# Keys and queries of an attention batch loaded ahead of its values, with block sums and value products later in TensorE's order

## The chip, the cores and the metric

One core of one Trainium2 chip runs the kernel. The metric is device time in microseconds (us) of one execution. The kernel before was run three times: 496.35, 497.45 and 497.51 us, median 497.45. The names of the profile are used: PE is TensorE, PEld its weight loads, DVE is VectorE, ACT is ScalarE, POOL is GpSimd, SP is SyncE, whose queue (SPq) issues nearly all DMAs of the attention stage.

## The reference

Three layers follow each other: an attention with a window and block summaries, a mixture of experts in which each token goes to one expert of limited capacity, and a second feed-forward layer with a gated softmax and a normalization. The change touches the attention alone. Batch is 2, heads 8, sequence 768, head dimension 64.

```python
k_sum = k.reshape(B, H, nb, block, D).max(axis=3)      # block = 32, nb = 24
v_sum = v.reshape(B, H, nb, block, D).mean(axis=3)
scores_l = scale * np.matmul(q, k.transpose(0, 1, 3, 2))
mask_l = np.abs(pos[:, None] - pos[None, :]) < window   # window = 16
scores_s = scale * np.einsum('bhsd,bhnd->bhsn', q, k_sum)
scores_s = scores_s + np.log(block)
scores_l_m = np.where(mask_l, scores_l, -1000000000.0)
scores_all = np.concatenate([scores_l_m, scores_s], axis=-1)
scores_all = scores_all - np.max(scores_all, axis=-1, keepdims=True)
a = np.exp(scores_all)
a = a / (np.sum(a, axis=-1, keepdims=True) + 1e-09)
v_all = np.concatenate([v, v_sum], axis=2)
return np.matmul(a, v_all).astype(np.float32)
```

Every query therefore sees its near keys and the 24 block summaries of all blocks; the product with the values takes the near values and the 24 block means of the values.

## The kernel before

The attention is cut into 24 units: 2 batches, 4 pairs of heads, 3 groups of four tiles of 64 queries. A unit passes three steps on TensorE. `score` (L332) multiplies the queries of two heads with 96 near keys and 24 block maxima; DVE adds the mask and takes the minimum (L338), ACT takes the exponential (L341). `attnT` (L348) transposes the weights and ACT copies them to a tile aT (L350). `pv` (L361) multiplies them with Vw, which holds for each tile 96 near values and in 24 further rows the block means; DVE divides by the sum (L364, L365, L368).

Before the first unit of a pair of heads, `prep` brings its keys and queries into the layout that the scores need, in three steps: DVE or POOL reorder the loaded keys kn into kr (L276), TensorE transposes keys (L292) and queries (L300), DVE copies the keys and takes block maxima (L294, L313), ACT copies the queries into qbd (L303), and DVE or POOL fill the summaries and margins of kTw (L315, L320, L321). Three pairs of such tiles exist, and three load buffers each for keys and queries.

The block means of the values come from `vsum`, once for a batch. Its first step sums the blocks by twelve products with all values of the batch (L255). Its second step lets ACT copy the sums (L259), moves them by one product to the right partitions (L261), lets ACT copy them again to a tile vs (L263), and issues eight DMAs on SP, one for each head (L265), that write them into the 24 rows of Vw. So a `pv` needs the values of its tiles and, of its own two heads, the two DMAs of L265.

TensorE and SP do what the code says in the order in which it says it: a table `plan` gives each step a place on a scale on which score u stands at u, and the steps are written out sorted by it. The order on DVE, ACT and POOL is made by the scheduler. What is written before the plan, as the first loads, stands first. In the plan of before, `pv` of unit u stands at the later of u + 3.5 and 5.3 + u/2, the two steps of `vsum` at 3.29 and 3.89 for batch 0 and at 12.65 and 13.25 for batch 1, and the loads of batch 1 among the units from 3 on.

When the attention ends, the tokens x go to memory (L372) and through `xT` (L382) and `logits` (L394) to the gating scores L. Then routing begins (`head`, L138 and following), after a memset (L823) in memory that the attention's tiles had held. During the last units three parts of the weight w_in are split into a high and a low half (`split64`, L70 to L79), with the tile ch between.

Of the kernel before, what the change touches and what calls it, by code (L numbers as in the profile page):

```python
# [8 lines left out]
F32 = mybir.dt.float32  # L9
F32R = mybir.dt.float32r  # L10
BF = mybir.dt.bfloat16
I32 = mybir.dt.int32
# [9 lines left out]
def tile_attention_moe_solu(ctx, tc, q, k, v, w_gate, w1, w2, w_in, w_out, g_ln, out):  # L22
# [6 lines left out]
    HP = H // 2  # L29
    NT = S // 64  # L30
    NBK = S // 32
    WIN = 96
    KEYS = WIN + NBK
# [29 lines left out]
    def split64(cv, raw, hi, lo, after=None, late=None):  # L63
        n = hi.shape[1]
        with tc.high_priority(-3000):
            y = cv.tile([128, n], F32, name="cy")
            h = cv.tile([128, n], I32, name="ch", bufs=2)

            with tc.issue_after(after.ins) if after is not None else nullcontext():
                nc.scalar.activation(y, raw[:, :, 1].bitcast(F32), AF.Abs, scale=2.0 ** -112)  # L70
            with tc.issue_after(late.ins) if late is not None else nullcontext():
                nc.vector.tensor_scalar(h, y.bitcast(I32), 3, 0x3FFFFFF8, op0=OP.logical_shift_left,
                                        op1=OP.bitwise_and)
            nc.vector.scalar_tensor_tensor(h, raw[:, :, 1], -0x40000000, h, op0=OP.bitwise_and, op1=OP.bitwise_or)
            nc.vector.scalar_tensor_tensor(h, raw[:, :, 0], 29, h, op0=OP.logical_shift_right, op1=OP.bitwise_or)
            h = h.bitcast(F32)
            nc.scalar.copy(hi, h)
            for c in range(0, n, 256):
                nc.gpsimd.tensor_tensor(lo[:, c:c + 256], h[:, c:c + 256], hi[:, c:c + 256].bitcast(F32), op=OP.subtract)  # L79
# [89 lines left out]
    cva = att.enter_context(tc.tile_pool(name="cva", bufs=1))  # L169
    ld = att.enter_context(tc.tile_pool(name="ld", bufs=3))  # L170
    vp = att.enter_context(tc.tile_pool(name="vp", bufs=1))
    wk = att.enter_context(tc.tile_pool(name="wk", bufs=2))
# [5 lines left out]
    def load_qk(b, hp):  # L178
        for nm, src in (("k", k), ("q", q)):
            t = ld.tile([128, 2, 3, 2 * D], F32, name=nm + "n")  # L180
            dma(t, src[b, 2 * hp:2 * hp + 2].rearrange("h (c p r) d -> p h c (r d)", c=3, r=2))
            nat[nm, b, hp] = t
# [3 lines left out]
    def load_v(b, t):  # L186
        lo = max(0, 64 * t - 16)
        hi = min(S, 64 * t + 80)
        o = lo - (64 * t - 16)
        dma(Vw[o:o + hi - lo, b, t, :, 0:D], v[b, :, lo:hi, :].rearrange("h p d -> p h d"))  # L190
# [23 lines left out]
    for i in range(NB):  # L214
        a = vp.tile([128, NT, KEYS], F32, name=f"kTw{i}")
# [8 lines left out]
    nc.vector.memset(Vw[0:32, :, 0, :, 0:D], 0.0)  # L224
    nc.vector.memset(Vw[64:96, :, NT - 1, :, 0:D], 0.0)
    load_qk(0, 1)
    for t in range(NT):
        load_v(0, t)
        if t == 5:
            load_qk(0, 2)  # L230
    for hp in range(3, HP):
        load_qk(0, hp)
    dma(wg, w_gate.rearrange("(k p) e -> p k e", p=128))

    nc.gpsimd.memset(Vw[:, :, :, :, D], 1.0)
# [108 lines left out]
    def attnT(u):  # L344
        s = ST.pop(u)
        p = pa.tile([128, 4, 128], F32, name="pA", bufs=2)
        for n in range(4):
            nc.tensor.transpose(p[0:KEYS, n, :], s[:, n, :], ident)  # L348
        a = wk.tile([KEYS, 4, 128], F32, name="aT", bufs=6)
        nc.scalar.copy(a, p[0:KEYS])  # L350
        AT[u] = a

# [48 lines left out]
    def at(u, f, *a):  # L401
        plan.setdefault(u, []).append((f, a))

    for u in range(NU):
        b, hp, g = units[u]
        i = b * HP + hp
        at(u, score, u)
        at(u + (2.2 if u < 21 else 1.9), attnT, u)
        at(max(u + (3.5 if u < 21 else 3.3), 5.3 + u / 2), pv, u)
    for i in range(1, B * HP):  # L410
        u0 = units.index((*divmod(i, HP), 0))
        for g in range(3):
            if i == 1:
                at(g + 0.4, prep, 0, 1, g)
            else:
                at(max(u0 + g - 4.5, g + 2.9), prep, *divmod(i, HP), g)
    for st in range(2):
        at(3.29 + 0.6 * st, vsum, 0, st)
        at(12.65 + 0.6 * st, vsum, 1, st)
    for b in range(B):  # L420
        for g in range(3):
            for n in range(2):
                u = units.index((b, HP - 1, g)) + (4 if b else 5.4)
                at(u + 0.7 * n + .6, xT, b * JB + 2 * g + n)
                at(u + 0.7 * n + 1.7, logits, b * JB + 2 * g + n)
    for t in range(NT):
        at(5 + t / 3, load_v, 1, t)
    for hp in range(HP):
        at(3 * hp + 3, load_qk, 1, hp)
    at(16, routing_consts)  # L430
    NCA = 3
    RAW64 = {}
# [5 lines left out]
    def split_in(cv, i, *after):  # L438
        kk, hf = divmod(i, 2)
        split64(cv, RAW64.pop(i), wiH[:, kk, 512 * hf:512 * hf + 512], wiL[:, kk, 512 * hf:512 * hf + 512], *after)  # L440
# [396 lines left out]
    def split_out(cv, i, after):  # L837
        split64(cv, RAW64.pop(8 + i), woH[:, i], woL[:, i], after)
# [53 lines left out]
    for ph in range(E):  # L892
        u = 540 if ph > WHOLE else 650
# [63 lines left out]
```

## Time and profile before

| what | value |
|---|---|
| median of three runs | 497.45 us |
| the profiled execution's own time | 498.66 us |
| its span, first to last instruction | 497.0 us |
| PE busy | 447.6 us, 90% of the span |
| PEld busy | 387.7 us, 78% |
| DVE busy | 274.3 us, 55% |
| ACT busy | 176.0 us, 35% |
| POOL busy | 89.0 us, 18% |
| chain that ended last | PE 71%, DVE 12%, DMA 6%, ACT 5% |
| mean granted clock of TensorE | 0.968 of full speed |

The attention fills about the first 104 us of the span, the routing of the first expert the stretch to 128 us, and the experts and the last layer the rest. The busy shares are means over stages with different limits. For a change in the attention the table says only that TensorE is busy most of the time; which engine ends last in that stage is read from the stretch itself.

### The profile page before, as it was taken

The numbers are of one execution on the slowest core, as the hardware profiler recorded it, in microseconds if no ns is written. First come the engines' busy times: TensorE is split into PE (matmuls) and PEld (weight loads), VectorE is DVE, ScalarE is ACT, GpSimd is POOL, SyncE is SP. The second block draws the span as 40 slices with busy tenths as digits, with TensorE's granted clock in tenths as the row PEclk, the third lists the DMA queues.
The fourth block names the chain that finished last, engine by engine and source line by source line (L and its number), as shares of the span: only waits on it lengthen the run. The fifth ranks groups of instructions, "written<-read, shape, count | busy, mean of one in ns | idle before, by whom it ended". The sixth has DMA issues, their size and how long they took to land.

```text
span 497.0 us, 9767 instructions
## 1 busy us (share of the span) xinstructions
PE 447.6 (90%) x3723; PEld 387.7 (78%) x3723; DVE 274.3 (55%) x1033; ACT 176.0 (35%) x425; POOL 89.0 (18%) x150
## 2 busy tenths in 40 slices
PE   2799999845778988999999999999999999999995
PEld 1668688634678868789888988988898899998773
DVE  7658577878594697675256526626662322213441
ACT  3578778711233432331321413123141313222331
POOL 9311200302324243202000200200020110100012
PEclk9999999975798998999999999999999999999999
DMA  9979861363869159008304800740390560000001
GB/s 195 195 158 207 220 181 40 109 231 131 272 218 368 54 180 316 1 2 279 113 1 137 257 21 1 243 149 1 118 275 30 179 205 1 1 22 1 22 21 42
DMA packets 92463, 64.61 MB, mean 130 GB/s; under 512 B 25728, under 2 KB 87168, under 8 KB 92416
## 3 DMA queue, kind: packets, MB, share of 16 engines
q1 hardware_dynamic: 90432, 57.70, 41.2%
q0 software_dynamic: 1984, 6.29, 3.5%
q8 instruction: 29, 0.48, 0.4%
q14 instruction: 18, 0.15, 0.1%
HBM read 56.51 MB, written 6.29 MB: 126 GB/s over the span
## 4 chain that ended last, share of the span: by engine, by line
PE 71%; DVE 12%; DMA 6%; ACT 5%; issue 3%; SPq 1%; POOL 0%; POOLq 0%; DVEq 0%; ACTq 0%
PE m L694 28%; PE h L759 13%; PE o L802 11%; PE pS L332 4%; PE pO L361 2%; DVE ge L124 2%; DMA xg<-xd,oidx 2%; PE pr L502 2%; PE pA L348 1%; DVE ex L768 1%; DMA wl<-in_moe_w_dram 1%; DMA kn<-in_k_dram 1%; PE tr L666 1%; ACT s L341 1%; PE T L255 1%
## 5 line engine op out<-in xcount | busy, mean ns | idle before, releaser
L694 PE MATMUL m<-xs,wr 128*128 128x192 f32 x384 | 79.7, 341 | 1.2 <-ACT xs L672 1.1
L694 PEld LDWEIGHTS m<-xs,wr 128*128 128x128 f32 x384 | 65.2, 195 | 6.2 <-ACT xs L672 1.4
L742 DVE TENSOR_TENSOR yl<-m,yh 128x128 fp32r<-128x128 f32 (+1 forms) x64 | 16.2, 253 | 82.1 <-ACT yh L741 82.1
L711 ACT ACTIVATE hT<-m 128x192 f32<-128x192 f32 x64 | 21.2, 331 | 90.0 <-PE m L694 76.6
L694 PE MATMUL m<-hT,wh 128*128 128x192 f32 x256 | 51.7, 332 | 0.0
L694 PE MATMUL m<-hT,wl 128*128 128x192 f32 x256 | 50.7, 335 | 0.0
L694 PEld LDWEIGHTS m<-hT,wl 128*128 128x128 f32 x256 | 45.0, 195 | 3.3
L694 PEld LDWEIGHTS m<-hT,wh 128*128 128x128 f32 x256 | 44.5, 193 | 3.7
L741 ACT CAST yh<-m 128x128 fp32r<-128x128 f32 (+1 forms) x64 | 15.2, 238 | 88.9 <-PE m L694 80.6
L341 ACT ACTIVATE s<-s,mx 128x120 f32<-128x120 f32 x96 | 31.5, 387 | 13.6 <-DVE mx L338 13.4
L759 PE MATMUL h<-wiH,yh 128*128 128x512 f32 x96 | 34.4, 446 | 0.0
L332 PE MATMUL pS<-kTw,qbd 128*128 128x120 f32 x192 | 27.8, 290 | 5.8 <-DVE kTw L315 4.8
L777 POOL TENSOR_TENSOR st<-st,mhalf 128x1 f32<-128x1 f32 x12 | 6.9, 574 | 144.8 <-DVE st L776 104.8
L759 PE MATMUL h<-wiL,yh 128*128 128x512 f32 x96 | 32.3, 424 | 0.0
L759 PE MATMUL h<-wiH,yl 128*128 128x512 f32 x96 | 32.2, 424 | 0.0
L802 PE MATMUL o<-woH,lh 128*128 128x512 f32 x96 | 30.8, 432 | 1.3 <-ACT lh L791 1.3
L802 PE MATMUL o<-woL,lh 128*128 128x512 f32 x96 | 32.0, 429 | 0.0
L332 PEld LDWEIGHTS pS<-kTw,qbd 128*128 128x128 f32 x192 | 24.8, 202 | 7.6 <-issue 6.0
L124 DVE TENSOR_TENSOR ge<-e,ios 128x1536 bf16<-128x1536 bf16 (+3 forms) x37 | 29.7, 803 | 0.8
L802 PE MATMUL o<-woH,ll 128*128 128x512 f32 x96 | 29.4, 418 | 0.0
L764 DVE TENSOR_REDUCE st<-h 128x1 f32<-128x1024 f32 x12 | 14.7, 1224 | 26.4 <-PE h L759 26.4
L338 DVE CUSTOM_DVE_ANT_0 s<-pS,mask 128x120 f32<-128x120 f32 x96 | 21.4, 278 | 12.4 <-PE pS L332 5.5
(184 smaller groups left out, 823.5 us busy)
## 6 DMA issues: line engine op xcount, KB each, us to landing
wr<-in_moe_w_dram SPq DMA_DIRECT2D x24, 512.0 KB
wl<-in_moe_w_dram SPq DMA_DIRECT2D x20, 512.0 KB
wh<-in_moe_w_dram SPq DMA_DIRECT2D x20, 512.0 KB
raw<-in_moe_w_in_dram SPq DMA_DIRECT2D x8, 512.0 KB
raw<-in_moe_w_out_dram SPq DMA_DIRECT2D x8, 512.0 KB
Vw<-in_v_dram SPq DMA_DIRECT2D x20, 192.0 KB
kn<-in_k_dram SPq DMA_DIRECT2D x8, 384.0 KB
qn<-in_q_dram SPq DMA_DIRECT2D x8, 384.0 KB
```

Source lines behind the costliest of these rows:

```text
L124: nc.vector.tensor_tensor(out, x.rearrange("p (j t) -> p j t", t=2)[:, :, None, :].to_broadcast([128, n // 2, b - a, 2]), ios[:, None, a:b ...
L332: nc.tensor.matmul(p[:, n, :], qbd[i][:, t, :], kTw[i][:, t, :], start=True, stop=True)
L338: nc.vector.tensor_tensor_reduce(s[:, n, :], p[:, n, :], m, scale=1.0, scalar=3.0e38, op0=OP.add, op1=OP.min, accum_out=mx[:, n:n + 1])
L341: EXPS[u] = nc.scalar.activation(s[:, n, :], s[:, n, :], AF.Exp, bias=mx[:, n:n + 1], scale=-1.0)
L361: nc.tensor.matmul(p[o:o + 64, n // 2, h, :], a[:, n, 64 * h:64 * h + 64], Vw[:, b, t, 2 * hp + h, :], start=True, stop=True)
L694: nc.tensor.matmul(p[:, :CAP], w[:, d, o:o + 128], rhs[:, d], start=d == 0, stop=d == n - 1)
L711: after(ph, "h", f, nc.scalar.activation(h[:, f], p[:, :CAP], AF.Relu))
L741: a = nc.scalar.copy(hi, s[:, s0:s0 + n])
L742: nc.vector.tensor_tensor(YL[k][:, d, c:c + n], s[:, s0:s0 + n], hi.bitcast(F32), op=OP.subtract)
L759: nc.tensor.matmul(ps, a[:, d, :], w[:, d, 512 * s:512 * s + 512], start=n == 0, stop=n == len(mm) - 1)
L764: nc.vector.tensor_reduce(st[:, 0:1], p, axis=AX.X, op=OP.max)
L802: nc.tensor.matmul(p, a[:, f, :], w[:, f, :], start=n == 0, stop=n == len(mm) - 1)
```

## The change

The diff, without unchanged parts:

```diff
-            h = cv.tile([128, n], I32, name="ch", bufs=2)
+            h = cv.tile([128, n], I32, name="ch", bufs=1 if cv is cva else 2)
...
     load_qk(0, 1)
-    for t in range(NT):
+    load_qk(0, 2)
+    for t in range(4):
         load_v(0, t)
-        if t == 5:
-            load_qk(0, 2)
-    for hp in range(3, HP):
-        load_qk(0, hp)
     dma(wg, w_gate.rearrange("(k p) e -> p k e", p=128))
...
-        a = wk.tile([KEYS, 4, 128], F32, name="aT", bufs=6)
+        a = wk.tile([KEYS, 4, 128], F32, name="aT", bufs=8)
...
-        at(max(u + (3.5 if u < 21 else 3.3), 5.3 + u / 2), pv, u)
+
+        at(max(u + (3.5 if u < 21 else 3.3), 9.05 + u / 2 if u < 12 else 10.1 + 0.57 * u), pv, u)
...
-                at(max(u0 + g - 4.5, g + 2.9), prep, *divmod(i, HP), g)
+                at(max(u0 + g - (4.5 if i < 4 else 3.4), g + 2.9), prep, *divmod(i, HP), g)
     for st in range(2):
-        at(3.29 + 0.6 * st, vsum, 0, st)
-        at(12.65 + 0.6 * st, vsum, 1, st)
+        at(7.63 + 0.6 * st, vsum, 0, st)
+        at(15.25 + 0.6 * st, vsum, 1, st)
...
+    at(0.02, load_qk, 0, 3)
+    for t in range(4, NT):
+        at(0.03, load_v, 0, t)
+    for i, u in ((4, 3), (5, 6), (6, 9.02), (7, 12)):
+        at(u, load_qk, *divmod(i, HP))
     for t in range(NT):
-        at(5 + t / 3, load_v, 1, t)
-    for hp in range(HP):
-        at(3 * hp + 3, load_qk, 1, hp)
+        at(9 if t < 6 else 9.03, load_v, 1, t)
```

The loads of the third pair of heads go ahead of the values of batch 0, and the fourth pair after the first four value tiles. The block sums of batch 0 go from behind score 3 to behind score 7, and the first product with the values from behind score 5 to behind score 9. In batch 1 the sums go from behind score 12 to behind score 15, and the products with the values stand later up to unit 15. Two more tiles aT hold the weights that wait for their product; the room comes from one tile ch.

On TensorE before, the place of the block sums of batch 0 and of the first product with the values. kr and qn are the keys and queries of a pair of heads, s the weights, comb the matrix of the second step; L255 and L261 are the two steps of the sums:

```order
L348 MATMUL pA<-ident,s 120x128 x4
L255 MATMUL T<-Vw,ind 32x512 x12
L261 MATMUL T<-s_358,comb 24x512
L292 MATMUL T<-ident,kr 128x128 x2
L300 MATMUL T<-ident,qn 128x128 x3
L332 MATMUL pS<-kTw_136,qbd_137 128x120 x4
L348 MATMUL pA<-ident,s 120x128 x4
L292 MATMUL T<-ident,kr 128x128 x4
L300 MATMUL T<-ident,qn 128x128 x3
L332 MATMUL pS<-kTw_136,qbd_137 128x120 x4
L348 MATMUL pA<-ident,s 120x128 x4
L361 MATMUL pO<-Vw,aT 64x65 x8
```

The same place on TensorE in the changed kernel (its lines are three lower: L252 and L258 are the sums, L358 is the product with the values):

```order
L252 MATMUL T<-Vw,ind 32x512 x12
L329 MATMUL pS<-kTw_142,qbd_143 128x120 x4
L345 MATMUL pA<-ident,s 120x128 x4
L258 MATMUL T<-s_523,comb 24x512
L289 MATMUL T<-ident,kr 128x128 x4
L329 MATMUL pS<-kTw_130,qbd_131 128x120 x4
L358 MATMUL pO<-Vw,aT 64x65 x8
L345 MATMUL pA<-ident,s 120x128 x4
L358 MATMUL pO<-Vw,aT 64x65 x8
```

Between the second step of the sums and the first product stood eight groups of products; now there stand two, the transposes of one key step and one score. A score and a transpose now stand between the two steps of the sums.

On DVE before, from the copies of the second pair's keys to the first mask operation of the first score:

```order
L276 COPY kr<-kn 128x3x128 x2
L294 COPY kTw_130<-T 128x8x64
L294 COPY kTw_130<-T 128x4x64
L313 TENSOR_REDUCE ks<-kTw_130 128x24
L320 COPY kTw_130<-kTw_130 128x11x16
L321 COPY kTw_130<-kTw_130 128x11x16
L315 COPY kTw_130<-ks 128x12x24
L338 ISA s,mx<-pS,mask_109 128x120
```

The same on DVE in the changed kernel:

```order
L273 COPY kr<-kn 128x3x128 x2
L291 COPY kTw_130<-T 128x8x64
L291 COPY kTw_130<-T 128x4x64
L273 COPY kr<-kn 128x3x128
L310 TENSOR_REDUCE ks<-kTw_130 128x24
L317 COPY kTw_130<-kTw_130 128x11x16
L318 COPY kTw_130<-kTw_130 128x11x16
L273 COPY kr<-kn 128x3x128
L312 COPY kTw_130<-ks 128x12x24
L335 ISA s,mx<-pS,mask_109 128x120
```

The two copies of the third pair's keys now stand among the operations that the first score waits for; before they stood behind the masks of score 1.

On SP in the changed kernel, the queue from the loads of the second half of batch 0 to the first loads of w_in:

```order
L262 DMA Vw<-vs 24x12x64 x8
L190 DMA Vw<-in_v_dram 80x8x64
L190 DMA Vw<-in_v_dram 96x8x64 x5
L181 DMA kn<-in_k_dram 128x6x128
L181 DMA qn<-in_q_dram 128x6x128
L190 DMA Vw<-in_v_dram 96x8x64 x5
L190 DMA Vw<-in_v_dram 80x8x64
L181 DMA kn<-in_k_dram 128x6x128
L181 DMA qn<-in_q_dram 128x6x128
L369 DMA xd<-x 128x2x512 x3
L60 DMA raw<-in_moe_w_in_dram 128x1024
L262 DMA Vw<-vs 24x12x64 x8
```

All values of batch 1 stand behind the eight DMAs of the sums of batch 0, as before, and those of the sums of batch 1 now stand behind two pairs of key and query loads, three stores of x and one load of w_in. Before, they stood behind three pairs and one store.

## Rows read from the trace of the kernel before

**Rows 1.** Busy time of each engine in stretches of 10 us, with columns.
```profile
core 0: us, PE busy (x) PEld busy (x) DVE busy (x) ACT busy (x) POOL busy (x), PEclk, DMA share, GB/s
20.00:30.00 10.00, 7.68 (x53) 3.65 (x52) 5.19 (x25) 6.78 (x16) 0.42 (x1) 1.00 1.26 220
30.00:40.00 10.00, 10.00 (x125) 8.90 (x125) 8.30 (x42) 9.40 (x23) 2.47 (x6) 1.00 0.55 113
40.00:50.00 10.00, 10.00 (x128) 9.04 (x126) 8.27 (x47) 8.76 (x24) 1.88 (x5) 1.00 1.10 209
50.00:60.00 10.00, 10.00 (x104) 6.28 (x104) 5.76 (x34) 7.72 (x19) 2.37 (x6) 1.00 1.02 249
```
**Rows 2.** TensorE in order of time, first score to first value product.
```profile
13.96 2.04 PE L332 MATMUL pS<-kTw,qbd 128*128 128x120 f32 x8 [4.77 <-DVE kTw L315]
...
20.99 0.66 PE L292 MATMUL T<-ident,kr 128*128 128x128 f32 x4 [0.20 <-ACT qbd L303]
22.68 1.12 PE L332 MATMUL pS<-kTw,qbd 128*128 128x120 f32 x8 [1.03 <-ACT qbd L303]
...
24.17 3.01 PE L255 MATMUL T<-Vw,ind 96*32 96x512 f32 x24
27.85 1.04 PE L261 MATMUL T<-s,comb 128*24 128x512 f32 x2 [0.67 <-ACT s L259]
...
29.56 0.55 PE L300 MATMUL T<-ident,qn 128*128 128x128 f32 x3 [0.30 <-ACT vs L263]
...
33.45 0.73 PE L361 MATMUL pO<-Vw,aT 120*64 120x65 f32 x16
```
**Rows 3.** TensorE in order of time, a steady stretch of units.
```profile
41.61 1.05 PE L332 MATMUL pS<-kTw,qbd 128*128 128x120 f32 x8
42.49 0.60 PE L348 MATMUL pA<-ident,s 128*120 128x128 f32 x4
43.02 0.73 PE L361 MATMUL pO<-Vw,aT 120*64 120x65 f32 x16
...
49.34 1.05 PE L332 MATMUL pS<-kTw,qbd 128*128 128x120 f32 x8
```
**Rows 4.** The end of the attention on TensorE, in order of time.
```profile
92.34 0.70 PE L361 MATMUL pO<-Vw,aT 120*64 120x65 f32 x16 [1.25 <-ACT s L341]
...
95.08 0.33 PE L382 MATMUL pA<-ident,x 128*128 128x128 f32 x1 [0.31 <-DVE x L368]
...
97.77 0.33 PE L382 MATMUL pA<-ident,x 128*128 128x128 f32 x1 [0.79 <-DVE x L368]
```
**Rows 5.** Pieces of the chain that ended last: start, us, what.
```profile
98.28 5.31 DMA xd<-x
...
124.61 3.01 DMA xg<-xd,oidx
```
**Rows 6.** VectorE in order of time, its copies of loaded keys.
```profile
8.07 3.02 DVE L276 COPY kr<-kn 128x384 f32<-128x384 f32 x2 [1.50 <-DMA kn<-in_k_dram]
...
19.12 0.74 DVE L276 COPY kr<-kn 128x384 f32<-128x384 f32 x2
...
27.30 0.75 DVE L276 COPY kr<-kn 128x384 f32<-128x384 f32 x2 [2.44 <-DMA kn<-in_k_dram]
```
**Rows 7.** ScalarE in order of time, last copy of the block sums.
```profile
28.93 0.58 ACT L263 COPY vs<-T 24x512 f32<-24x512 f32 x1 [1.13 <-PE T L261]
```
**Rows 8.** The issues of the block sums' DMAs on SP.
```profile
29.53 6.97 SPq L265 DMA_DIRECT2D Vw<-vs  x8
```
**Rows 9.** VectorE in order of time, the split of w_in (L74, L75).
```profile
94.94 0.68 DVE L74 SCALAR_TENSOR_TENSOR ch<-raw,ch 128x512 int32<-128x512 int32 x1
...
95.65 0.69 DVE L75 SCALAR_TENSOR_TENSOR ch<-raw,ch 128x512 int32<-128x512 int32 x1
```
**Rows 10.** Engines by stretch at the end of the attention and in routing.
```profile
88.00:98.00 10.00, 7.65 (x108) 6.13 (x103) 8.57 (x36) 7.13 (x17) 4.21 (x6) 1.00 0.30 107
107.00:117.00 10.00, 2.80 (x55) 1.93 (x55) 6.71 (x35) 0.66 (x1) 0.00 (x0) 0.50 0.40 143
```

## The prediction

> **What bounds the kernel now.** I read the busy time in stretches first. From 30 to 60 us TensorE is busy for 10.00 of 10.00 us in every stretch, while ScalarE has 7.72 to 9.40 and VectorE less [rows 1]; so from there the attention lasts as long as TensorE's work, and a new order gains nothing in that stretch. From 20 to 30 us TensorE has 7.68: here an order can gain. The second view is TensorE in order of time [rows 2]. After the first score at 13.96 us it stands for 0.20 and 1.03 us (queries that ScalarE copies), then, around the block sums, 0.67 us (ScalarE's copy of the sums) and 0.30 us. That is 2.20 us in all until the first value product at 33.45 us. The block sums themselves (3.01 and 1.04 us) stand early, but they are work and not waits; moving them moves it. The third view is the end of the stage [rows 4]: 1.25, 0.31 and 0.79 us, together 2.35 us. The stage ends with the last tokens' store, 5.31 us from issue to landing, behind which the chain goes on into routing [rows 5]; beside it run the last transposes and gating scores. Everything after that is one chain through routing, which the change doesn't touch, so a shift of the attention's end is passed on whole. At most 2.20 + 2.35 = 4.55 us can be gained, if no new wait comes.
>
> **The change part by part**, as time of TensorE until the attention's end.
>
> *Loads.* The keys of the third pair land before the values, and with them the 2.44 us goes for which VectorE stood for the fourth pair's keys [rows 6]. That wait ended no wait of TensorE of its own, since TensorE was at the block sums meanwhile; its worth is in the 0.30 us above. The price is on VectorE's order: the two copies of the third pair's keys now stand before the first score. In their old place they took 0.74 us [rows 6], so the first score comes 0.7 us later. The least is 0, the most 3.0 us, as two such copies took at 8.07 us, where POOL worked beside them. I take 0.7, since it is the same pair's row.
>
> *Block sums later.* With a score and a transpose between the steps, ScalarE's copy is covered: 0.67 and 0.30 us go, and I count the 0.20 with them: -1.2. The 1.03 us stay, for the first queries' copies stand as they did.
>
> *Units without value products.* A steady unit takes (49.34 - 41.61) / 3 = 2.58 us on TensorE, of which the value product is some 0.7 [rows 3]; without it 1.9. ScalarE has 8.76 us of work in 10 us [rows 1], so 2.25 us for a unit. In the five units from score 3 to the sums, TensorE would run ahead by at most 5 x 0.35 = 1.8 us. The transposes stand 2.2 units behind their score, which absorbs most of it; what is left is that a transpose of queries needs a buffer that ScalarE empties. Bounds 0 and 1.8; I take 0.6, about one copy by ScalarE as in rows 7.
>
> *First value product.* It needs the means of its two heads in Vw. Before, from the end of the second step (27.85 + 1.04 = 28.89 us) to the product at 33.45 us passed 4.56 us [rows 2]. Eight groups of products filled them, so TensorE did not stand. In these 4.56 us lie ScalarE's copy, 0.58 us [rows 7], and two issues of 6.97 / 8 = 0.87 us each [rows 8], after the second of which the landing follows. The bounds of that path are 0.58 + 2 x 0.87 = 2.3 us, if landing were free, and 4.56. Nearest in kind is the small gather, 3.01 us from issue to landing [rows 5]: 0.58 + 0.87 + 3.01 = 4.5, which I take. In the changed order only a key step (0.66 [rows 2]) and a score (49.34 - 41.61 is three units; score to transpose 42.49 - 41.61 = 0.88 [rows 3]) stand between: 1.5 us. New wait: 4.5 - 1.5 = 3.0 us (bounds 0.8 and 3.1). Behind the waiting product stand all other steps of TensorE; ScalarE and VectorE run dry, for their next scores come from there. The products of units 1 and 2 need no more DMAs, and from unit 3 the DMAs have had a unit's time for each.
>
> By this wait TensorE works in some 7 of 10 us, as at the end of the stage, where it had 7.65 of 10 us and the granted clock stayed at 1.00; with 2.80 of 10 in routing it was 0.50 [rows 10]. I therefore add nothing for the clock. The Trainium skill (TensorE: Matmul & The Clock Gate, "The HAM clock gate") says that the array's clock follows how busy it was recently and halves when it idles, which speaks against this change; the row at 88 us shows gaps without such a fall, that at 107 us shows the fall. By the page alone one would add work at half speed behind the wait, which the first rival below prices.
>
> *Sums of batch 1.* The copy of the sums frees a buffer that the second query transpose behind it needs: 0.5 us, from 0.58 [rows 7] (bounds 0 and 0.6). Then seven groups stand before the first product of batch 1: a score, two transposes of x and two gating scores, a transpose, queries. At 0.88 for the score, 0.53 for a transpose (43.02 - 42.49 [rows 3]) and some 0.4 for the small ones this is 3.5 us against 4.5: 1.0 us of wait. On top may come the queue of transfers. From the end of batch 0's issues, near 46 us, twelve value tiles (10 x 192 + 2 x 160 KB), four key or query loads of 384 KB, and three stores and one load of 512 KB stand ahead: 5.8 MB, at 209 to 249 GB/s [rows 1] 24 to 28 us, so they land between 70 and 74 us. TensorE comes to the place at about 72 us. The wait lies between 0 and 3.3 us; I take 1.2.
>
> *End of the stage.* ScalarE now copies the last two transposed weight tiles ahead of the third part of the split, and VectorE does the second split behind the value products: I count the 1.25 and the 0.31 us as gone, and half of the 0.79. Against it the third split's two operations, 0.68 and 0.69 us [rows 9], now stand within the head of routing: +1.0 after their overlap with the store. Together -0.9 (bounds -2.35 and +1.4).
>
> The sum: 0.7 - 1.2 + 0.6 + 3.0 + 0.5 + 1.2 - 0.9 = +3.9 us. The profiled execution took 498.66 us, its span 497.0 and 1.7 around it, and lies 1.2 us above the median of 497.45; I add the sum to both: 502.6 for such an execution, 501.4 for the median. The tiles aT and the smaller ch cost nothing else: two more aT are what eight waiting units need, and the one ch only binds the splits to each other, counted at the end.
>
> **The rivals.**
> *A heavier wait.* The 3.0 us stop brings the clock to its lower level for a stretch, or the copies before the first score take their 3.0 us. For it: the fall in routing, and the row at 8.07 us. Against it: 1.00 with 7.65 of 10 busy. Doubled work for as long as the stop costs 3 us more: 504.4. Chance 0.10.
> *An exchange.* Without the transfers' queue (-1.2), with ScalarE's lag absorbed (-0.6) and the end at half of its bound (-0.3), 1.8 us are left, and if landing takes 1 us less than the gather's, 0.8: 498.2, no difference that can be told. For it: the small sum of waits on both sides. Chance 0.20.
> *Faster.* ScalarE was the second bound, with 6.78 of 10 us before 30 us and 9.40 after [rows 1]. Eight units of exponentials before the first value product use its idle time, and later no unit waits for ScalarE: all waits at the end go (-2.35) with the early ones (-1.2), and the first product finds its means because ScalarE's lag lets TensorE come there late. 0.7 - 3.55 + 0.5 = -2.4: 495.1. It decides from a wait at the first product under some 0.7 us. Against it: TensorE is back to back from 30 us already, so ScalarE isn't what it waits for, and a late arrival is itself time. Chance 0.17.
> The forecast has 0.53.
>
> **How the numbers follow.** A measurement tells a difference from about 0.3%, 1.5 us. The forecast and the heavier wait are slower: 0.63. The exchange is the same: 0.20. The rest is faster: 0.17. The range goes from 496.6, which takes in the exchange and leaves the faster case out, to 504.8 with the heavier wait.
>
> **What would show it.** Right: the first score near 14.7 us; no wait at the sums' second step; one wait of TensorE of about 3 us at the first value product, put down to the DMAs of the sums or to nothing that the profile shows; one of 1 to 3 us at the first product of batch 1; the last store some 4 us later. Wrong: a first value product without a wait, or waits at the end that vanish altogether; or a routing that shifts by another amount than the last store, for then the later stages answer too. If the clock falls in the attention, the first rival holds.

## The result and the profile after

The changed kernel took 504.49 us (median of four runs, 501.83 to 506.09), the kernel before, with one run more than was shown, 497.48 us. The ratio is 1.0139, 95% interval 1.0092 to 1.0186: 4.6 to 9.3 us slower. The forecast was 501.4 us with a range of 496.6 to 504.8. The profiled execution took 504.62 us, its span 502.9 against 497.0. One later run, of e1 at 509.93 us, was in the slower state that some executions of a kernel show; it is left out of its median and ratio.

TensorE after, in order of time from the first score to the first value product (start us, us, engine, line, operation, in brackets the idle time before it and what ended it). Lines of the attention are three lower than before: L358 is the value product, L252 and L258 the block sums.

```profile
14.48 2.03 PE L329 MATMUL pS<-kTw,qbd 128*128 128x120 f32 x8 [5.29 <-DVE kTw L312]
...
23.48 1.12 PE L329 MATMUL pS<-kTw,qbd 128*128 128x120 f32 x8 [1.15 <-ACT qbd L300]
...
27.93 0.55 PE L297 MATMUL T<-ident,qn 128*128 128x128 f32 x3 [0.58 <-ACT qbd L300]
...
30.74 0.55 PE L297 MATMUL T<-ident,qn 128*128 128x128 f32 x3 [0.72 <-ACT qbd L300]
...
34.19 2.79 PE L252 MATMUL T<-Vw,ind 96*32 96x512 f32 x24
...
39.18 1.04 PE L258 MATMUL T<-s,comb 128*24 128x512 f32 x2 [0.68 <-ACT s L256]
...
43.60 0.33 PE L358 MATMUL pO<-Vw,aT 120*64 120x65 f32 x2 [1.91 <-DMA Vw<-vs]
44.51 1.14 PE L358 MATMUL pO<-Vw,aT 120*64 120x65 f32 x14 [0.57 <-DMA Vw<-vs]
...
48.85 1.90 PE L329 MATMUL pS<-kTw,qbd 128*128 128x120 f32 x8
...
104.47 0.66 PE L379 MATMUL pA<-ident,x 128*128 128x128 f32 x4 [0.47 <-ACT xT L384]
...
112.08 0.34 PE L503 MATMUL pr<-oh,ge 128*16 128x8 bf16 x8 [1.11 <-DVE L L393]
```

Against [rows 2] the reader sees four things. The first score is 0.52 us later. The wait of 0.30 us behind the sums is gone, but that of 0.67 us at their second step is there as before, and two waits of 0.58 and 0.72 us for ScalarE's query copies are new. The first value product waits 1.91 and then 0.57 us for the sums' DMAs: together the 2.48 us that take the place forecast at 3.0. And the score at 48.85 us takes 1.90 us, where [rows 3] have 1.05. Why shows the view by stretches (busy us with instruction counts, then the granted clock, DMA share and GB/s):

```profile
core 0: us, PE busy (x) PEld busy (x) DVE busy (x) ACT busy (x) POOL busy (x), PEclk, DMA share, GB/s
30.00:40.00 10.00, 8.60 (x69) 5.43 (x68) 4.40 (x31) 9.71 (x24) 2.84 (x7) 1.00 0.24 61
40.00:44.00 4.00, 2.02 (x15) 1.55 (x14) 1.59 (x9) 2.79 (x8) 0.00 (x0) 1.00 0.17 35
44.00:51.00 7.00, 6.49 (x53) 5.71 (x55) 2.82 (x9) 1.61 (x3) 1.04 (x3) 0.51 0.49 101
51.00:60.00 9.00, 9.00 (x137) 7.85 (x134) 7.20 (x43) 6.44 (x17) 0.96 (x2) 1.00 1.29 223
```

From 30 to 40 us ScalarE is the engine that works all the time (9.71 of 10), where TensorE was in [rows 1]. TensorE then stands for about half of the stretch from 40 to 44 us, and behind that stop the granted clock is 0.51, the lower of its two levels (1.2 GHz), while TensorE has full work. Before, the clock was 1.00 all through the attention.

Where the time to the first routing product (112.08 against 103.51 us) comes from, worked out from all TensorE rows between: its idle time and its work from the first score to the end of the last value product, and the rest. "Again" are second profiles of the unaltered kernels, from the experiments.

| profile | first score | idle | work | last product to routing | first routing product |
|---|---|---|---|---|---|
| before | 13.96 | 3.87 | 78.24 | 7.44 | 103.51 |
| before again | 12.24 | 3.70 | 78.48 | 7.81 | 102.23 |
| after | 14.48 | 6.83 | 82.10 | 8.67 | 112.08 |
| after again | 14.23 | 7.20 | 78.79 | 7.75 | 107.97 |

### The profile page after: what moved, and what is told of

Same layout as the page of the kernel before. It is cut to its first block, busy times and chain, and to the rows that moved or that the text cites. A ratio compares the mean times of both kernels' runs of the same rounds, so it can differ in the third digit from the quotient of the medians.

```text
span 502.9 us, 9771 instructions
## 1 busy us (share of the span) xinstructions
PE 448.3 (89%) x3723; PEld 388.6 (77%) x3723; DVE 275.9 (55%) x1033; ACT 176.3 (35%) x425; POOL 87.0 (17%) x150
## 4 chain that ended last, share of the span: by engine, by line
PE 66%; DVE 12%; ACT 8%; DMA 5%; issue 4%; SPq 2%; POOL 1%; POOLq 0%; DVEq 0%; ACTq 0%
PE m L695 27%; PE h L760 13%; PE o L803 11%; PE pS L329 3%; ACT s L338 3%; PE pO L358 2%; DMA xg<-xd,oidx 2%; DVE ge L124 2%; PE pr L503 2%; DMA kn<-in_k_dram 1%; ACT qbd L300 1%; DMA wl<-in_moe_w_dram 1%; PE pA L345 1%; DVE ex L769 1%; SPq L631 1%
## 5 line engine op out<-in xcount | busy, mean ns | idle before, releaser
L695 PE MATMUL m<-hT,wh 128*128 128x192 f32 x256 | 50.6, 327 | 0.0
L695 PE MATMUL m<-hT,wl 128*128 128x192 f32 x256 | 49.0, 327 | 0.0
L695 PEld LDWEIGHTS m<-hT,wl 128*128 128x128 f32 x256 | 43.4, 189 | 3.2
L329 PEld LDWEIGHTS pS<-kTw,qbd 128*128 128x128 f32 x192 | 26.1, 211 | 8.9 <-issue 8.7
```

The source lines that it names most:

```text
L329: nc.tensor.matmul(p[:, n, :], qbd[i][:, t, :], kTw[i][:, t, :], start=True, stop=True)
L695: nc.tensor.matmul(p[:, :CAP], w[:, d, o:o + 128], rhs[:, d], start=d == 0, stop=d == n - 1)
```

## The experiments

Times are medians; every ratio compares the mean with that of runs of the kernel before on the same chip, with its 95% interval. The kernel before took 496.3 to 498.0 us on these chips, so versions are compared by their ratios. "Wait" is the idle time of TensorE at the first value product, "routing" the start of the first routing product. "Half clock" is the time at the lower clock, before and after 100 us of the span: the sum of 5 us x 2 x (1 - granted clock) over stretches of 5 us from 10 to 300 us. It counts time at the lower level, not what that costs.

| kernel | us | ratio | first score | wait | routing | half clock |
|---|---|---|---|---|---|---|
| before | 497.48 | | 13.96 | 0 | 103.51 | 0 + 30.7 |
| before again (e9) | 497.97, one run | | 12.24 | 0 | 102.23 | 0 + 34.1 |
| after | 504.49 | 1.0139 [1.0092, 1.0186] | 14.48 | 2.48 | 112.08 | 6.8 + 27.3 |
| after again (e5) | 504.51 | 1.0142 [1.0093, 1.0191] | 14.23 | 2.48 | 107.97 | 0 + 34.1 |
| e1, wait filled | 505.28 | 1.0113 [1.0049, 1.0176] | 14.47 | 0.21 | 107.64 | 0 + 37.6 |
| e2, sums early | 500.64 | 1.0058 [1.0024, 1.0093] | 14.22 | 0.26 | 104.96 | 0 + 34.2 |
| e3, loads only | 499.52 | 1.0035 [1.0004, 1.0066] | 14.47 | 0 | 104.08 | 0 + 34.2 |
| e4, two ch | 506.01 | 1.0173 [1.0136, 1.0211] | 14.50 | 2.48 | 109.70 | 6.8 + 27.2 |
| e6, orders only | 506.24 | 1.0172 [1.0111, 1.0233] | 12.27 | 3.63 | 112.74 | 10.3 + 27.3 |
| e7, sums late | 511.91 | 1.0304 [1.0242, 1.0367] | 14.47 | 9.51 | 117.76 | 10.2 + 27.3 |
| e8, copies on POOL | 497.78 | 1.0040 [1.0003, 1.0077] | 13.40 | 0.26 | 105.71 | 0 + 27.4 |
| e10, small dose | 505.49 | 1.0162 [1.0117, 1.0208] | 14.23 | 2.87 | 110.37 | 3.4 + 34.1 |
| e11, copies on ScalarE | 499.53 | 1.0057 [1.0030, 1.0084] | 12.26 | 0.25 | 104.59 | 0 + 34.1 |
| e12, values first | 497.92 | 1.0031 [1.0011, 1.0050] | 12.24 | 0.25 | 104.26 | 0 + 34.1 |

**e1: the wait filled with work.** Ten products that nothing reads, ahead of the first value product:

```
+    def busy(n):
+        p = pa.tile([128, 512], F32, name="T", bufs=2)
+        for i in range(n):
+            nc.tensor.matmul(p[:, 0:128], ident, ident, start=True, stop=True)
...
     def pv(u):
         b, hp, g = units[u]
         a = AT.pop(u)
+        if u == 0:
+            busy(10)
```

> The changed kernel with ten products that nobody reads (identity by identity, some 2.5 us) on TensorE ahead of the first value product: the wait for the block sums stays, but TensorE is busy in it. Theory of the clock: of the changed kernel's loss, some 2.5 us is the wait itself and some 3.9 us the granted clock of 0.5 behind it, from 44 to 51 us. Then the clock stays at 1.00 there, the first value product comes at about 44 us as before, and the time is 3 to 4 us under the changed kernel's, about 501. Rival: the extra busy time of TensorE comes from its new order and not from the clock; then nothing moves, 504 to 505.

The products took 2.50 us (from 40.83 us) and the wait was 0.21 us; the clock stayed at 1.00 until 106.2 us, and routing began 4.4 us earlier than after. But the time was not better, against the theory's 501, and its half-clock stretches behind 100 us were 37.6 us. In this profile the fall is gone with the stop; in the next run it is gone with the stop left whole, so that the products kept the clock up is not shown.

**e5: the changed kernel again**, unaltered.

> The changed kernel once more, unaltered, to see which of its readings repeat. Theory: the waits are set by its order, so the wait at the first value product comes again at 2.3 to 2.7 us, the first score at 14.3 to 14.7 us, and the last transposes' and the routing's head's waits within 0.3 us. The granted clock behind the wait falls to 0.5 in some executions and not in others: chance one half here; with the fall the first routing product starts near 112 us, without it near 108 to 109.5. Rival: the fall belongs to this order whatever the run, so it comes again with the product at 112 us. Time 503.5 to 505.5 on either, since later stages' half-clock stretches move the other way.

TensorE again, at the first value product and at the start of routing:

```profile
43.28 0.33 PE L358 MATMUL pO<-Vw,aT 120*64 120x65 f32 x2 [1.91 <-DMA Vw<-vs]
44.17 0.69 PE L358 MATMUL pO<-Vw,aT 120*64 120x65 f32 x14 [0.57 <-DMA Vw<-vs]
...
107.97 0.34 PE L503 MATMUL pr<-oh,ge 128*16 128x8 bf16 x8 [1.44 <-DVE L L393]
```

```profile
40.00:50.00 10.00, 7.52 (x101) 6.47 (x101) 6.07 (x30) 5.98 (x16) 1.03 (x3) 1.00 0.38 79
```

The waits at the value product are the same to 0.01 us and the clock did not fall: same order, same stop, 2.52 of 5 us busy from 40 to 45 us in both (from 40 to 50 us 7.52 in both, with a clock of 0.71 after). The fall is a matter of the execution. Routing came 4.1 us earlier here, the end of the span only 1.3 us (501.6 against 502.9). The 2.8 us between can be placed: e5 has two stretches at the lower level, 3.4 us each, that the first profile of after lacks. First after, then e5:

```profile
160.00:165.00 5.00, 3.46 (x23) 3.02 (x21) 2.68 (x8) 1.53 (x5) 1.89 (x3) 1.00 1.11 367
190.00:195.00 5.00, 3.20 (x29) 2.50 (x28) 5.00 (x21) 1.14 (x4) 1.24 (x2) 1.00 0.94 304
```

```profile
160.00:165.00 5.00, 4.10 (x20) 3.97 (x19) 0.89 (x3) 1.95 (x5) 1.41 (x2) 0.70 1.10 376
190.00:195.00 5.00, 3.11 (x33) 2.63 (x32) 4.97 (x19) 1.02 (x3) 2.58 (x3) 0.77 1.09 377
```

Its lead on TensorE is 4.5 us at 150 us of the span, 2.8 at 169 and 1.4 at 221: 1.7 and 1.5 us go where these stretches lie. So in this pair each fall has its price; after paid for one in the attention and e5 for two behind it, and the sum of half clock is 34.1 us in both.

**e2: sums early.** After, with the sums of batch 0 about where they cover the path:

```
-        at(7.63 + 0.6 * st, vsum, 0, st)
+        at(6.03 + 0.6 * st, vsum, 0, st)
```

> The changed kernel with the block sums of batch 0 at 6.03 and 6.63 instead of 7.63 and 8.23, all else as it is: between their second step and the first value product then stand two scores, three transposes and a key step, about 4.4 us, as long as the sums need to get into place. Theory of wait and clock: the wait of 2.5 us shrinks to under 0.5, the clock stays at 1.00, and 5 to 6 us of the loss go: 498 to 500. Rival, that the loss lies in the loads and the late order of all value products: only the wait goes, 502.

The wait shrank to 0.26 us, routing began 3.0 us earlier than in e5 (2.2 of it this wait, 0.7 that at the sums' second step, which is gone), and the ratio fell from 1.0139 to 1.0058; the time lies between the theory's 498 to 500 us and the rival's 502. The late place of the sums is the largest single part of the loss, and 0.2 to 0.9% remain without it.

**e7 and e10: sums later**, the same line with 8.44 and with 8.39.

> The changed kernel with the two steps of the sums of batch 0 directly before the first value product (8.44 and 9.04 in place of 7.63 and 8.23), the opposite direction of the run with early sums. Theory: the cover between the second step and the product was a key step of 0.66 us and a score of 0.88 to 1.05, in sum 1.6; without it the wait at the first value product grows from 2.5 to about 4.0 us, the clock falls behind it in its profile, and time is 505.5 to 507.5. Rival (the wait is not the path's but the DMA queue's, busy with values and keys at that moment): the wait stays near 2.5 us and the time with it.

Both theories failed: the wait was 9.31 and then 0.20 us. At 9.04 the second step had come behind the twelve value loads of batch 1, which stand at 9 and 9.03, and a pair of keys and queries at 9.02; SP issues in the order of the code. Its last issues up to the sums' in e7:

```profile
37.73 0.81 SPq L181 DMA_DIRECT2D qn<-in_q_dram  x1
38.58 7.37 SPq L190 DMA_DIRECT2D Vw<-in_v_dram  x6
46.05 6.78 SPq L262 DMA_DIRECT2D Vw<-vs  x8
```

The eight issues of the sums started at 46.05 us, as the loads were out. ScalarE's copy for them was ready at 42.56 us (41.98 + 0.58), and after, with a free queue, the issues began 0.02 us behind that copy: 3.5 us of the wait are the queue. The transfers were slower too: from the first issue to the value product 5.2 us here, with a DMA share of 1.24 meanwhile, against 2.7 us after, with 0.18. The dose had moved more than one thing. e10 keeps SP's order and takes only the key step out of the cover:

> The changed kernel with the two steps of the sums of batch 0 at 8.39 and 8.99 in place of 7.63 and 8.23, so that between the second step and the first value product only one score (0.9 to 1.1 us) is left and no key step, with SP's order unchanged: the small dose that the run before, in which the sums' DMAs also fell behind six value loads, was not. Theory (path of sums to values): the wait grows by the key step that leaves, 0.5 to 0.7 us, from 2.5 to 3.0 to 3.2 us. Rival (it depends on what else the DMAs carry): the wait stays near 2.5 us. Time 504.5 to 506 on the theory, 504 to 505 on the rival.

```profile
39.77 1.04 PE L258 MATMUL T<-s,comb 128*24 128x512 f32 x2 [0.22 <-ACT s L256]
...
44.19 0.33 PE L358 MATMUL pO<-Vw,aT 120*64 120x65 f32 x2 [2.30 <-DMA Vw<-vs]
45.10 0.99 PE L358 MATMUL pO<-Vw,aT 120*64 120x65 f32 x14 [0.57 <-DMA Vw<-vs]
```

The wait grew by 0.39 us to 2.87, less than the 0.5 to 0.7 expected and in the theory's direction; the time, 505.49 us, fits it. From the start of the second step to the value product it is 4.42 us here (44.19 - 39.77), as after (43.60 - 39.18) and in e5: with queue and DMAs free the path keeps its length, and the wait is that length less the cover. Beside other transfers it is longer, 6.15 us in e6 (46.48 - 40.33). The key step, now ahead of the second step, takes that step's wait from 0.68 to 0.22 us, but a wait of 1.04 us for ScalarE's exponentials is new at 35.92 us.

**e3 and e6: loads and orders apart.** e3 is before with the new place of the loads of batch 0 alone; the new places of batch 1's loads stand in neither of the two runs:

```
-    for t in range(NT):
+    load_qk(0, 2)
+    for t in range(4):
         load_v(0, t)
...
+    at(0.02, load_qk, 0, 3)
+    for t in range(4, NT):
+        at(0.03, load_v, 0, t)
```

> The kernel before with the new order of loads in the first half alone (third pair of keys and queries ahead of the values, fourth pair behind four value tiles), sums and value products where they were. If the loads are paid for by the sums, TensorE waits for the last values at the sums of batch 0, 3 to 4 us, perhaps with a fall of the clock, and the first score comes 0.5 us later: 500 to 503. Rival: the keys that VectorE no longer waits 2.4 us for are worth as much as the values' delay: 497 to 498.

The first score came at 14.47 us, the sums' waits stood as in [rows 2] (0.68 and 0.30 us) without the 3 to 4 us of the theory, and it cost 0.35%, more than the rival allowed. e6 is after with the loads of before, and only the new places of sums, products and preparations:

> The changed kernel with the load order of before, so that only the order of sums, value products, preparations and the two tile counts is changed; it completes the square with the run that has only the loads. Theory (the path from the sums to the first value product costs, whatever the loads): wait there 2.0 to 2.7 us, first score back at 14.0, time 502 to 504.5, +4 to +6 over before. Rival A (loads and orders only hurt together, since batch 1's loads and the late key copies collide): within 1.5 us of before. Rival B (the loads carry it): 498 to 499.

```profile
12.27 2.03 PE L332 MATMUL pS<-kTw,qbd 128*128 128x120 f32 x8 [3.08 <-DVE kTw L315]
...
27.98 1.14 PE L292 MATMUL T<-ident,kr 128*128 128x128 f32 x4 [3.27 <-DVE kr L276]
...
46.48 1.47 PE L361 MATMUL pO<-Vw,aT 120*64 120x65 f32 x16 [3.63 <-DMA Vw<-vs]
```

It lost as much as the whole change, and none of its three theories had it whole. With values loaded first TensorE stands 3.27 us for the third pair's keys, the wait that the loads of the change avoid, and the sums' transfers run beside loads of batch 1 (DMA share 0.88; 4.2 us from first issue to product against 2.7 after), which makes the wait 3.63 us. The loads thus serve the orders: undoing them all gains nothing, though those of batch 0 cost something by themselves. What I had not looked for is the 12.27 us of the first score: earlier than before's, with the same loads.

**e9: the kernel before again**, unaltered, to see whether 13.96 us was its own.

> The kernel before, unaltered, for a second profile of it. In its first profile VectorE's second key copy ended together with an operation of POOL that took 2.21 us (8.88 to 11.09 us), where the run with only the orders changed, which has the same work at that place, shows that operation with 0.28 us and its first score at 12.27 us. Theory: the 2.21 us is a matter of the execution and not of the kernel, so the first score comes at 12.2 to 12.6 us here, and the true price of the third pair's copies ahead of it is about 2 us and not the 0.5 us that the first two profiles show. Rival: it belongs to the order of before, and the first score is again at 13.9 to 14.0 us. Everything behind the first score as in the first profile: sums' waits 0.6 to 0.7 and 0.3 us, first routing product 89.5 us after the first score.

```profile
12.24 2.03 PE L332 MATMUL pS<-kTw,qbd 128*128 128x120 f32 x8 [3.06 <-DVE kTw L315]
```

```profile
8.88 0.28 POOL L101 TENSOR_SCALAR_AFFINE_SELECT others<-ones 128x128 bf16<-128x128 bf16 x1
9.12 0.09 POOL L108 MEMSET masks<- 128x1 int32 x1
9.17 2.22 POOL L109 IOTA ios<- 128x384 bf16 x1
```

The theory held. In the first profile of before the same POOL operation took 2.21 us, and VectorE's key copy, the 3.02 us in [rows 6], ended with it:

```profile
8.88 2.21 POOL L101 TENSOR_SCALAR_AFFINE_SELECT others<-ones 128x128 bf16<-128x128 bf16 x1
```

Here the two copies took 1.49 us (from 7.41). That one execution had stood for 1.7 us ahead of its first score; it was also 1.2 us over its median. In the thirteen other profiles that POOL operation takes 0.28 us. The price of the third pair's copies is 14.22 to 14.50 less 12.24, 2.0 to 2.3 us.

**e8, e11 and e12: taking the costs out.** All have the early sums of e2. e8 puts the third pair's two copies on POOL:

```
-                e = nc.gpsimd if b * HP + hp >= 4 else nc.vector
+                e = nc.gpsimd if b * HP + hp >= 4 or b * HP + hp == 2 else nc.vector
```

> The changed kernel with early sums of batch 0 (as in the run before that had them) and the two key copies of the third pair on POOL in place of VectorE. Theory: these two copies are what moved the first score from 13.96 to 14.48 us, so it comes back to 13.8 to 14.1, the attention ends 0.5 us sooner and the time is 0.5 us below that of early sums alone: 499.5 to 500.5. Rival (POOL working beside VectorE slows the copies that are left, as in the row of 1.75 us for one copy at 10.03): first score at 14.5 or later, no gain.

The first score came at 13.40 us, better than expected, and the ratio is 1.0040; whether it beats e2's 1.0058 can't be told from the intervals. It also shows the wait that I had forecast for the first product of batch 1 and that after doesn't have:

```profile
13.40 2.03 PE L329 MATMUL pS<-kTw,qbd 128*128 128x120 f32 x8 [4.20 <-DVE kTw L312]
...
72.53 0.30 PE L358 MATMUL pO<-Vw,aT 120*64 120x65 f32 x2 [1.12 <-DMA Vw<-vs]
73.04 0.69 PE L358 MATMUL pO<-Vw,aT 120*64 120x65 f32 x14 [0.22 <-DMA Vw<-vs]
```

e11 puts the copies on ScalarE, behind the first pair's queries (`first`), and the sums of batch 1 at 14.55:

```
+                third = b * HP + hp == 2
+                with tc.issue_after(nat["first"].ins) if third else nullcontext():
+                    (nc.scalar.copy if third else e.tensor_copy)(
...
-        at(7.63 + 0.6 * st, vsum, 0, st)
-        at(15.25 + 0.6 * st, vsum, 1, st)
+        at(6.03 + 0.6 * st, vsum, 0, st)
+        at(14.55 + 0.6 * st, vsum, 1, st)
```

> A version that takes the found costs out of the changed kernel: sums of batch 0 at 6.03 and 6.63, sums of batch 1 at 14.55 and 15.15 in place of 15.25 and 15.85, and the third pair's two key copies on ScalarE behind the first pair's queries. Theory: the copies waited on VectorE for POOL's operation of 2.22 us at 9.2 us; on ScalarE, which stands idle there, they cost nothing, so the first score comes at 12.2 to 12.6 us, the wait of 1.12 us at the first product of batch 1 shrinks to 0.4 us or less, and the first routing product comes at 102.5 to 104 us; time 496 to 498, no difference to before or a little faster. Rival (VectorE is held up by POOL in the next operation instead): first score at 13.3 us or later, time 498 to 500.

```profile
10.68 0.92 ACT L275 COPY kr<-kn 128x384 f32<-128x384 f32 x2
```

```profile
12.26 2.03 PE L332 MATMUL pS<-kTw,qbd 128*128 128x120 f32 x8 [3.08 <-DVE kTw L315]
...
57.42 2.77 PE L252 MATMUL T<-Vw,ind 96*32 96x512 f32 x20
60.52 1.95 PE L252 MATMUL T<-Vw,ind 96*32 96x512 f32 x4 [0.32 <-DMA Vw<-in_v_dram]
```

The first half held: the two copies took 0.92 us there, and the first score came at 12.26 us. The 2 us were not kept: the sums of batch 1 now stood ahead of their last values and took 5.05 us (57.42 to 62.47) in place of 2.79, and the time missed its range by 1.5 us. e12 takes that out by one pair's keys and queries behind the values:

```
-    for i, u in ((4, 3), (5, 6), (6, 9.02), (7, 12)):
+    for i, u in ((4, 3), (5, 6), (6, 9.04), (7, 12)):
```

> The version with the third pair's key copies on ScalarE, early sums of batch 0 and sums of batch 1 at 14.55, with one thing more: the twelve value loads of batch 1 stand on SP's queue ahead of one pair's keys and queries and no longer around them. In the run before, the sums of batch 1 started at 57.42 us and waited for the last value load: their 24 products took 5.05 us (57.42 to 62.47) against 2.79 us without a wait. Theory (the 2 us gained at the first score were lost there): the sums take 2.8 to 3.2 us, the first routing product comes 1.9 to 2.4 us sooner, at 102.2 to 102.7 us, and the time equals before within 0.3%, 496 to 498. Rival (all transfers of that stretch are bound by the DMAs' rate, and the keys that now come later stop TensorE instead): a new wait for kn or qn, first routing product at 103.5 us or later, time 498.5 to 500.

```profile
57.26 2.78 PE L252 MATMUL T<-Vw,ind 96*32 96x512 f32 x24
...
70.97 0.30 PE L361 MATMUL pO<-Vw,aT 120*64 120x65 f32 x2 [1.34 <-DMA Vw<-vs]
71.49 0.69 PE L361 MATMUL pO<-Vw,aT 120*64 120x65 f32 x14 [0.22 <-DMA Vw<-vs]
```

The sums were whole again, but the product behind them met their DMAs (1.34 and 0.22 us, beside a DMA share of 0.99), so that routing moved by 0.33 us only. Neither theory had named that wait. The ratio of 1.0031, 1.0011 to 1.0050, is the nearest to before, and none of these versions beats that kernel.

**e4: two ch, seven aT**, for the end of the stage.

```
-            h = cv.tile([128, n], I32, name="ch", bufs=1 if cv is cva else 2)
+            h = cv.tile([128, n], I32, name="ch", bufs=2)
...
-        a = wk.tile([KEYS, 4, 128], F32, name="aT", bufs=8)
+        a = wk.tile([KEYS, 4, 128], F32, name="aT", bufs=7)
```

> The changed kernel with two tiles ch as before and seven aT instead of eight. In the order on VectorE the third part of the split then stands ahead of the last copies again and not within the head of routing. Theory: the single ch costs the end of the attention 1 to 2 us, by two operations of 0.68 us and the copies behind them that POOL slows; then 1 to 2 us less than the changed kernel, 502.5 to 503.5, with the waits at the first value product unchanged. Rival: the end hangs on the last store of x and nothing changes, 504.5.

A wait of 1.27 us for ScalarE stood again in the last products (at 99.01 us), as the one of 1.25 us in [rows 4], and routing began 7.48 us after the last product, against 8.67 after and 7.75 in e5. The time was not better. That the one ch costs the end 1 to 2 us fell: it trades one wait for another. A wait of 0.66 us for the sums' DMAs also stood at the first product of batch 1, which e5 doesn't have. Its clock is one more case beside e5: behind a stop of the same 2.48 us it stayed at 1.00 (its 6.8 us of half clock lie ahead, at 12.8 to 19.6 us).

## Why the prediction was right, and where its terms were not

The direction and the main mechanism held: the wait at the first value product, put down to the sums' DMAs, and worth more than the waits removed. The size held less well. The medians differ by 7.0 us, where the forecast was 3.9; the measured 504.49 us lies 0.3 us inside the range, next to the 504.4 of the rival "a heavier wait" and in part on its grounds, dearer copies and more time at the lower clock, though neither cost the 3 us that it priced. So that the range held is in part luck. Against e9, the undisturbed profile of before, e5 is the plain case: its routing starts 5.74 us later (first score 1.99, idle 3.50, work 0.31, the end -0.06) and its span ends 5.3 us later. By the terms that is 2.0 - 0.3 + 1.6 + 2.5 + 1.1 - 1.5, with 0.3 of work: three terms fell short by 3.2 us in all, three others were too dear by 1.7 us, and the errors cancel in part. Term by term:

- *First score*, +0.7: measured 2.0 to 2.3. The step that failed is "I take 0.7, since it is the same pair's row". [rows 6] had its price at a place where POOL stood still. Ahead of the first score a copy meets POOL's operation of 2.22 us, and its keys land late as well. VectorE after, and POOL beside it:

```profile
10.03 1.75 DVE L273 COPY kr<-kn 128x384 f32<-128x384 f32 x1 [0.37 <-DMA kn<-in_k_dram]
...
13.34 0.78 DVE L273 COPY kr<-kn 128x384 f32<-128x384 f32 x1
```

```profile
9.16 2.22 POOL L109 IOTA ios<- 128x384 bf16 x1
```

The copy of 10.03 us ends at 11.78, just behind POOL's operation (11.38), and in seven further profiles, where it starts between 9.80 and 10.42 us, it ends between 11.67 and 11.81. The Trainium skill (SBUF — State Buffer, "SBUF: two separate sides") says that GpSimd and a VectorE operation in a two-port performance mode, to which it counts an fp32 copy from SBUF to SBUF, take one pair of ports as an exclusive lock, and that whichever comes second stands until the other's whole instruction is over. These ends agree. In e9, without these copies, VectorE works beside the same POOL operation (9.17 to 11.39 us):

```profile
9.86 0.95 DVE L313 TENSOR_REDUCE ks<-kTw 128x24 f32<-128x768 f32 x1
10.73 0.77 DVE L320 COPY kTw<-kTw 128x176 f32<-128x176 f32 x1
```

The reduction takes what it takes where POOL stands still (0.95 us from 20.23 in the first profile of before), and only the small copy L320, 0.29 us in e5 (there L317), is held, by 0.5 us; e11, where ScalarE copies the keys, has two like rows (0.95 and 0.78 us). So of the 2.0 us in e5 some 0.9 are POOL's (its first copy takes 1.32 us; the two of [rows 6] took 0.74 together), 0.5 the wait for the keys to land, and the rest the copies themselves. The upper bound of 3.0 us came from a row that e9 didn't repeat; that it covers the measured 2.0 to 2.3 is luck.
- *Waits around the sums*, -1.2: measured -0.3. "ScalarE's copy is covered" failed: 0.68 us stayed at the second step, because ScalarE had 9.71 of 10 us of work: the sums ended on TensorE at 36.98 us (34.19 + 2.79), but their copy stood behind other work of ScalarE:

```profile
37.69 0.96 ACT L338 ACTIVATE s<-s,mx 128x120 f32<-128x120 f32 x3
38.56 0.57 ACT L256 COPY s<-T 128x512 f32<-128x512 f32 x1
```

Only the 0.30 went; in e2 the copy comes up at once and the second step has no wait.
- *Units without value products*, +0.6: measured 1.3 in the waits of 0.58 and 0.72 us for query copies, and 0.1 to 0.3 in the one at 23 us. Right in kind and inside its bounds of 0 and 1.8; ScalarE, not TensorE, set the pace there.
- *First value product*, +3.0: measured 2.48, and by e2 and e10 it is the path less its cover. Counted as the forecast did, from the end of the second step, the path was 3.38 us to the first head's product and 4.29 to the second's (4.5 forecast); the cover was 1.48 (1.5 forecast). Of the 4.56 us before, TensorE stood for 0.30, so they were not quite filled.
- *The clock*, 0: in the attention wrong for the profile after, where the work rose by 3.86 us, and right for e5. In the whole span the half-clock time was 34.1 us in the profiles of after, e5 and e9 alike, but not in all runs on record: by the mean granted clock the kernel before spent 32.5 us at the lower level (62 runs beside the experiments), the changed kernel 37.5 us (the eight runs of after and e5). At the 1.5 to 1.7 us that 3.4 us cost in e5, these 5.0 us are worth some 2 us, an estimate. The Trainium skill (TensorE: Matmul & The Clock Gate, "The HAM clock gate") says that the clock follows how busy the array was recently. The profiles of after, e6, e7 and e10 agree, in which a stop was followed by the lower level (0.50); in e5 and e4, with an equal stop of 2.48 us, it stayed at 1.00. The rival "a heavier wait" has its fall here in some executions.
- *Batch 1*, +0.5 and +1.2: after shows 0.42 us at the query transpose and none at the product; 0.67 us is new behind a copy of x. The product's wait is there in e8 (1.34), e12 (1.56) and e4 (0.66) and not in e1, e2 and e11; what decides it is not shown.
- *End*, -0.9: the waits that are 1.25 and 0.31 us in [rows 4], 1.26 and 0.18 in e9, are gone; from the last product to routing passes 0.06 us less in e5 than in e9. So -1.5 in e5; after, where that last stretch takes 0.9 us more, -0.6.

The medians differ by 7.0 us, the profiles by 5.3 (e5 to e9) and 5.9 us, since the profiles don't stand for the middle: e5's execution is the fastest of its four, e9's 1.4 us above the median of the other runs of before on its chip. Much of the scatter goes with the clock: of the 62 runs of before the 36 with a mean clock of 0.968 or more took 496.3 us on average, the 26 below it 498.3. Together with the clock's 2 us the profiles' 5.3 come to the 7.3 us between the means of these runs. What stays open is why the changed kernel spends more time at the lower level, and why two equal stops have different sequels: the half clock of the profiles is 37.5 or 37.6 us in e1, e6, e7 and e10, 30.7 in before and 27.4 in e8.

## What to carry to other kernels

A producer that reaches its consumer through a copy, a queue and a DMA has a path whose length can be read: write it down (4.42 us here with queue and DMAs free, 6.15 beside other loads, 10.36 behind them on the queue) and see that as much work stands between them in the engine's order, and also what a move puts ahead of it on the queue. Price a moved copy by rows from the place to which it goes, with what the other engines do there, not by its old place. And take a second profile of the kernel before, when a row of it (3.02 for a copy of 1.49 us) doesn't fit its neighbours.

## What the runs showed of the hardware

A copy on VectorE stood until POOL's operation of 2.22 us was over, while a reduction on VectorE ran beside it unhindered (0.95 us). In one execution of before and in no other profile, a POOL operation of 0.28 us took 2.21 us beside a copy that took 1.5 us longer; both were slow, and why is not shown. The lower clock came behind a stop of 2.48 us in one execution and not in another of the same kernel. Small transfers of the sums took 2.7 us from first issue to use with the DMAs nearly idle (share 0.18) and 4.2 and 5.2 us beside loads (0.88 and 1.24). A score next to a value product costs TensorE a little: score to product 0.98 us (46.64 to 47.62 in e5), where score to transpose was 0.88 in [rows 3].
